# Half of the second pair's input loaded before the first pair's ticks, and an identity matrix loaded six ticks earlier

## The chip, the core and the metric

The kernel runs on one core of a Trainium2 chip. The metric is the device time of one execution in microseconds (us). The engines of the core are named as the profile names them: PE is the matrix engine (its weight loads are shown as PEld), DVE the vector engine, ACT the scalar engine, POOL and SP two more engines that here mainly issue DMA transfers. A `q` behind a name (SPq, POOLq) is the part of an engine that issues.

## The reference

What is computed, for `x` of 8 batch entries, 5696 positions and 128 channels:

```python
def _attn_ref(x, h):
    L = 2 * S
    Xf = np.fft.rfft(x, n=L, axis=1)
    Hf = np.fft.rfft(h, n=L, axis=0)
    return np.fft.irfft(Xf * Hf[None, :, :], n=L, axis=1)[:, :S, :]

def _moe_ref(x, w_r, w_i, w_ch):
    X = np.fft.rfft(x, axis=1)
    Y = np.zeros_like(X)
    Xr, Xi = np.real(X[:, :64]), np.imag(X[:, :64])
    Yr = einsum('bmd,mde->bme', Xr, w_r) - einsum('bmd,mde->bme', Xi, w_i)
    Yi = einsum('bmd,mde->bme', Xr, w_i) + einsum('bmd,mde->bme', Xi, w_r)
    Y[:, :64] = Yr + 1j * Yi
    u = x + np.fft.irfft(Y, n=S, axis=1)
    return u + np.maximum(u @ w_ch, 0.0)
```

The first function is a causal convolution along the sequence with one filter per channel. The second takes its result, multiplies the lowest 64 Fourier modes by a 128x128 complex matrix each, adds the inverse transform to the result, and ends with a residual ReLU product with `w_ch`. Inputs and output are float32; the kernel works in float16 with float32 accumulation.

## The kernel before

All transforms are matrix products. A position is split as s = 64 q + p, with 89 values of q and 64 of p. The spectrum is worked through in 90 classes; four classes make a tick, so a pass over all classes has 23 ticks (0 to 22). Two batch entries make a pair, and the program goes through four pairs one after the other.

**Input.** `Xin` holds the pair's x, with q on the partitions. It comes in eight pieces of 16 values of p each (`XN`), four for each of the two entries. A piece is brought from DRAM by two DMAs issued by POOL (`x_load`: 80 rows and 9 rows, float32 in DRAM and float16 on arrival) into a staging place, and then copied by one DVE instruction into `Xin` (`x_place`, L362), which can't happen before the last first-stage matmul of the pair before has read `Xin`. The first pair's pieces are staged as `Xr`, which lies over the first part of the tile `Hs`. The later pairs' pieces are staged as `Xt`, eight places that lie over the front of the tile `As`; piece i covers eight classes of it, those of ticks 2i and 2i + 1.

**First stage** (`a_tile`, 32 of them for each pair): products of `Xin` with `F`, moved out of PSUM into `As` by ACT and DVE in turn. A tile needs all of `Xin`. Six of the next pair's tiles are drawn into the last ticks of a pair (the table `border`), the first at tick 22.

**Ticks.** In tick t, `second` multiplies `As` with the constant `M` for four classes, ACT moves the result to `Xs`, DVE multiplies it by the filter's spectrum `Hs` into one of three buffers `U` (L617 and L625), PE multiplies the product of two ticks earlier by `Wc`, ACT moves that into a slot of `Zs` or `Zt`, SP writes the slot to DRAM (`zscr`), and PE multiplies a slot of one tick earlier by `G` for the 64 modes. During the first pair's ticks the filter's own spectrum is built too, six ticks ahead (`filter_tick`, `LH` = 6, so in ticks 0 to 16): PE makes it from `Ah` and `M`, DVE moves it into the first half of `Hs` (L312), and two DMAs issued by SP copy it, with its halves of partitions swapped, into the second half. The product of a tick needs all three to have arrived.

**Tick order.** Each engine's program is a list in the order in which the Python code adds to it, and every engine works its list strictly in order, SP's and POOL's DMA issues included. Waits are made from reads and writes of named tokens. In `tick(g_, t)` the order is: `x_place` of the pieces due at t, `second`, `products`, the loads for the next pair, the `Wc` products and the write to `zscr`, the `G` products, `filter_tick`.

**Input of the next pair, before the change.** At the even ticks 2 to 16 of a pair, piece t/2 - 1 is loaded into its place over `As`, after the tick's products and `second` are done. For the second pair the copies stand at ticks 9, 10, 12, 15, 16, 18, 20 and 22 of the first (`XPLACE[0]`).

**Last pair and after.** During the last pair's ticks the dictionary `early` issues loads for what follows: mode weights `W`, tables `S4a`, `S4b` and `IBs`, and chunks `ZT0` to `ZT3` read back from `zscr`. The identity matrix `Id` is loaded by SP at tick 20; its place lies over one of the `Zt` slots 8 and 9, which the last pair uses once only, at ticks 8 and 9, so it waits for those slots' readers (`after=ZY`). After the ticks PE mixes the modes (`XT` with `W`), DVE and ACT move the result to `Y`, PE transposes it with `Id` (L808), ACT and DVE move that to `C`, and then the output stage runs: per tile, products of `ZT` with `S4` and of `C` with `IBs` into `UT`, then products with `w_ch`, ReLU, sum, and writes of the output by SP.

Of the kernel before, what the change touches and what calls it, by code (L numbers as in the profile page):

```python
# [5 lines left out]
F16 = mybir.dt.float16  # L6
# [117 lines left out]
def bass_long_conv_fft__then__afno_spectral_mix_kernel(nc, x, h, moe_w_r, moe_w_i, moe_w_ch, out):  # L124
    B, S, D = x.shape
# [3 lines left out]
    NQ = S // J  # L129
    assert NQ * J == S  # L130
    L = 2 * S
    NK = NQ + 1
    NP = B // 2
    KT = 4
# [71 lines left out]
    def at(name, cols, dt, off):  # L206
        return nc.alloc_sbuf_tensor_at(name, [P, cols], dt, offset=off)
# [7 lines left out]
    AW, HW, GW = NK * 2 * D, NK * D, (NK // 2 + 1) * P  # L215
# [8 lines left out]
    a_h = take(2 * HW * 2)  # L224
# [4 lines left out]
    NU, NXS, NZ, NZX = 3, 2, 6, 10  # L229
# [7 lines left out]
    XC = 4  # L237
    XN = J // XC
    XB = XN * D
    x_all = at("Xr", 2 * XC * XB, F16, a_h)  # L240
    x_st = [at(f"Xt{i}", XB, F16, a_as + i * XB * 2) for i in range(2 * XC)]
    u_s = [at(f"U{i}", 2048, F16, a_st + i * 4096) for i in range(NU)]
    x_s = [at(f"Xs{i}", 1024, F16, a_st + NU * 4096 + i * 2048) for i in range(NXS)]
    z_s = [at(f"Zs{i}", 1024, F16, a_st + NU * 4096 + (NXS + i) * 2048) for i in range(NZ)] + \
# [44 lines left out]
    def pv(bank, off, dims, p0=0, n=P):  # L289
        return bass.AP(ps, p0 * 4096 + bank * 512 + off, [[4096, n]] + [list(d) for d in dims])  # L290
# [5 lines left out]
    def bank(i):  # L296
        return ("bank", i)
# [3 lines left out]
    def evac(dst, src, reads, writes, scale=None, eng=None, after=()):  # L301
        e = eng
        if e is None:
            turn[0] ^= 1
            e = "scalar" if turn[0] else "vector"
        if e == "scalar":
            if scale is None:
                R.add(e, lambda h_: h_.copy(dst, src), reads, writes, after=after)  # L308
            else:
                R.add(e, lambda h_: h_.activation(dst, src, COPY, scale=scale), reads, writes, after=after)  # L310
        elif scale is None:
            R.add(e, lambda h_: h_.tensor_copy(dst, src), reads, writes, after=after)  # L312
        else:
            R.add(e, lambda h_: h_.tensor_scalar_mul(dst, src, scale), reads, writes, after=after)  # L314
# [9 lines left out]
    def once(key, toks):  # L324
        if key in first:
            return []
        first[key] = 1
        return list(toks)
# [32 lines left out]
    def x_place(i, src, toks):  # L361
        R.add("vector", lambda e: e.tensor_copy(bass.AP(x_sb, i * XN * XS, [[XW, NQ], [XS, XN], [1, D]]),  # L362
                                                src),
              list(toks) + XZ, [("xin", i)])
# [107 lines left out]
             [bank(t), bank(t + 1)], [("as", j)], 1.0 / 64, eng=eng, after=once(("hp", j), HP))  # L472


    def filter_tick(t, banks):
        n = len(ticks[t])
        hb = banks
        for i, k in enumerate(ticks[t]):
            for r in range(2):
                for dh in range(2):  # L480
                    mm(pv(hb[dh], i * DH, [[1, DH]]),
                       ap(m_sb, MW, J * dh, J, k * 3 * J + (J if r == 0 else 0) + dh * J, [[1, P]]),
                       ap(ah_sb, HW, J * dh, J, (2 * k + r) * DH, [[1, DH]]), r == 0, r == 1,
                       AHT + mtok(k) + [("ag", k)], [bank(hb[dh])])
        lo, hi = KT * t * D, (KT * t + n) * D
        old = once("xr", [t_ for r_ in XR for t_ in r_]) if t == 0 else []
        evac(h_sb[:, lo:hi], pv(hb[0], 0, [[DH, n], [512, 2], [1, DH]]), [bank(hb[0]), bank(hb[1])], [("h", t, 0)],
             eng="scalar" if t < LH and t != 2 else "vector",
             after=old)
        for p0, p1 in ((0, J), (J, 0)):  # L490
            dma("sync", h_sb[p0:p0 + J, HW + lo:HW + hi], h_sb[p1:p1 + J, lo:hi], "s", [("h", t, 0)], [("h", t, 1, p0)])
        if t % 2 and t // 2 < NG:
            s0, s1 = t // 2 * GP, min(t // 2 * GP + GP, NS)
            dma("sync", g_sb[:, s0 * P:s1 * P], bass.AP(c_g, s0 * P, [[GW, P], [1, (s1 - s0) * P]]), "c", (),
                [("g", t // 2)], after=[("ag", k) for k in range(s0, s1)])
# [24 lines left out]
    def clear_zt(i):  # L520
        z32 = zt[i][1][0:PB, :].bitcast(U32)
        R.add("gpsimd", lambda e: e.memset(z32, 0), (), [("zt0", i)], after=list(zt_old[i][1]) + pace)
# [13 lines left out]
    def load_s4(part):  # L536
# [6 lines left out]
    early = {3: lambda: load_w(2), 5: lambda: load_w(3), 8: lambda: load_s4(1),  # L543
             10: lambda: clear_zt(0),
             11: lambda: load_zt(0, "gpsimd"),
             14: lambda: clear_zt(1),
             15: lambda: load_zt(1, "gpsimd"),
             16: lambda: load_s4(0),
             18: lambda: load_ib(),
             20: lambda: load_id(),  # L550
             NT - 2: lambda: (load_zt(2, "gpsimd", SLACK), load_zt(3, "gpsimd"), clear_zt(2), clear_zt(3))}
    pace = []
    SLACK = [("zd", NP - 1, s_) for s_ in range(NT - NZL)]
# [1 line left out]
    def load_id():  # L555
        dma("sync", id_sb[:, :], bass.AP(c_w, 2 * P, [[3 * P, P], [1, P]]), "c", (), [("id",)], after=ZY)
# [47 lines left out]
    def products(g_, t, sl):  # L604
# [15 lines left out]
        if not straight(g_, t):  # L620
            e = onchip.get((g_, t))
            if e is None:
# [2 lines left out]
        R.add("vector", lambda e: e.tensor_tensor(uv, src, hv, MULT),  # L625
              bk + [("h", t, 0), ("h", t, 1, 0), ("h", t, 1, J)], [("u", i)])

    Z_OLD = [("ag", k) for k in range(NS, NS + 8 * (NZX - NZ))]
    XPLACE = [9, 10, 12, 15, 16, 18, 20, 22], [9, 10, 13, 14, 17, 18, 20, 22]

    def zroom(g_, s_):
        if g_ == NP - 1:
            return s_ if s_ < NZX else (s_ - NZX) % NZL
        return (s_ - 2 * NZ) % NZX if g_ == 0 and s_ >= 2 * NZ else s_ % NZS[g_]

    def xtok(n):
        return [("xt", n, p_) for p_ in range(2)]

    def tick(g_, t):
        if g_ + 1 < NP:  # L640
            for i in range(2 * XC):
                if t == XPLACE[g_ > 0][i]:
                    x_place(i, bass.AP(x_st[i], 0, [[XB, NQ], [D, XN], [1, D]]), xtok(i))
        with_h = with_h_at(g_, t)
        if t < NT:
            of_two = t > 0 and twin(g_, t - 1)
            if not of_two:
                second(g_, t)
            products(g_, t, slot_of(g_, t))
            if twin(g_, t):  # L650
                second(g_, t + 1)
                if straight(g_, t):
                    copied(g_, t + 1, slot_of(g_, t + 1))
        drain = list(border[t]) if t in border and g_ + 1 < NP else []
        if drain and t >= NT:
            j, sl, e = drain.pop(0)
            a_tile(j, [sl], e)
        if g_ + 1 < NP and t % 2 == 0 and 0 < t <= 4 * XC:
            i = t // 2 - 1
            x_load(g_ + 1, i, x_st[i], xtok(i), [("u", t % NU)] + AST)  # L660
        if LC <= t < NT + LC:
            s_ = t - LC
            n = len(ticks[s_])
            i, zi = s_ % NU, zroom(g_, s_)
            zb = [turns("z", ZBANK) for b in range(2)]
            for b in range(2):
                for r in range(2):
                    mm(pv(zb[b], 0, [[1, n * D]]), (W1, W2)[r], u_s[i][:, r * 1024 + b * 512:r * 1024 + b * 512 + n * D],
                       r == 0, r == 1, [("u", i), ("wc",)], [bank(zb[b])])
                evac(bass.AP(z_s[zi], b * D, [[1024, P], [2 * D, n], [1, D]]),  # L670
                     pv(zb[b], 0, [[D, n], [1, D]]), [bank(zb[b])], [("zs", zi, b)], eng="scalar",
                     after=once(("zx", zi, b), Z_OLD) if zi >= NZ else ())
            zo = (g_ * NK + KT * s_) * P * 256
            dma("sync", bass.AP(zs, zo, [[256, P], [P * 256, n], [1, 256]]),
                bass.AP(z_s[zi], 0, [[1024, P], [256, n], [1, 256]]), "z",
                [("zs", zi, 0), ("zs", zi, 1)], [("zd", g_, s_)])
            if drain and t >= NT:
                j, sl, e = drain.pop(0)
                a_tile(j, [sl], e)
        if LM <= t < NT + LM:  # L680
            s_ = t - LM
            zi = zroom(g_, s_)
            for i, k in sorted(enumerate(ticks[s_]), key=lambda q: (s_ > 0 or q[1] != 1, q)):
                for b in range(2):
                    if k % 2:
                        o, off, n, sl = pv(MB, b * P, [[1, P]]), (k + 1) // 2 * P, P, (k + 1) // 2
                    else:
                        ms, off = even[k]
                        n, sl = 2 * len(ms), 0
                        dims = [[M, 2]] if len(ms) == 1 else [[ms[1] - ms[0], 2], [M, 2]]  # L690
                        o = pv(MB, b * P + ms[0], dims)
                    mm(o, z_s[zi][:, i * 256 + b * P:i * 256 + b * P + P], g_sb[:, off:off + n],
                       k == 1 and b == 0, k == NK - 1 and b == 1, [("g", sl // GP), ("zs", zi, b)], [bank(MB)])
        if drain and t < NT + LM - 1:
            j, sl, e = drain.pop(0)
            a_tile(j, [sl], e)
        if with_h:
            filter_tick(t + LH, [2, 3])

    FOUR = [0, 2, 4, 6]  # L700
    for j in range(32):
        a_tile(j, FOUR)
# [217 lines left out]
```

## Time and profile before

| | us |
|---|---|
| three timed executions | 385.3, 388.07, 394.62 |
| their median | 388.07 |
| the profiled execution | 392.56 |
| its span, first to last instruction | 390.3 |

The profiled execution's time is 2.26 us over its span; that remainder lies outside the instructions. Its mean granted clock was 0.981.

| engine | busy us | share of the span |
|---|---|---|
| PE | 361.9 | 93% |
| ACT | 310.9 | 80% |
| DVE | 303.4 | 78% |
| PEld | 278.7 | 71% |
| POOL | 84.8 | 22% |

In the trace the first pair's first stage runs from 27 to about 44 us, its ticks from there to about 93, the second pair's part to about 149, the third's to about 204, the fourth's ticks end at about 262, and the output stage runs from about 274 to the end. Busy time says where an engine works, not whether the end depends on it; for that the chain of work that ended last and the idle time before an instruction are read, stretch by stretch. A DMA is seen in two places: the issue on the queue of its engine, and the time at which it landed.

### The profile page before, as it was taken

To read this page: it belongs to the slowest core of one execution; us is meant where nothing else is said; L and a number is where in the kernel's file an instruction comes from. 1 tells how busy PE (TensorE), PEld (TensorE's weight loads), DVE (VectorE), ACT (ScalarE), POOL (GpSimd) and SP (SyncE) were. 2 spreads that over 40 slices of the span, in tenths; PEclk is the share of its full clock that TensorE was granted. 3 is DMA by queue.
4 is the path that set the end of the run, shared out by engine and by line. 5 is a ranking of instruction groups with operands and counts; after the bars stand their busy time and mean duration, and the time that the engine had idled before them with its cause. 6 is when DMAs were issued, how large, how long until landed. Compare 5 with 4: busy or idle time off the path is not lost.

```text
span 390.3 us, 12468 instructions
## 1 busy us (share of the span) xinstructions
PE 361.9 (93%) x5346; PEld 278.7 (71%) x5346; DVE 303.4 (78%) x346; ACT 310.9 (80%) x489; POOL 84.8 (22%) x134
## 2 busy tenths in 40 slices
PE   7889899988989999989999899995999999999993
PEld 7878766655856667856667666665898988988872
DVE  3649889977998998989999988763437767777785
ACT  8469599987889997899997899992457676777784
POOL 8700022310643210832213213346000000000000
PEclk9999999999999999999999999996899999999997
DMA  7997489998899996999995899999889999999767
GB/s 147 210 307 303 127 164 269 253 250 253 85 137 200 241 265 176 121 122 238 244 274 113 125 313 360 352 368 396 316 322 364 359 414 412 410 403 372 293 269 304
DMA packets 87202, 103.94 MB, mean 266 GB/s; under 512 B 22884, under 2 KB 72676, under 8 KB 83592
## 3 DMA queue, kind: packets, MB, share of 16 engines
q1 hardware_dynamic: 62667, 67.76, 50.3%
q0 software_dynamic: 24480, 35.40, 43.1%
q8 instruction: 42, 0.69, 0.7%
q14 instruction: 13, 0.10, 0.1%
HBM read 70.61 MB, written 51.12 MB: 312 GB/s over the span
## 4 chain that ended last, share of the span: by engine, by line
PE 67%; DMA 12%; DVE 7%; ACT 5%; POOL 3%; issue 2%; SPq 1%; DVEq 0%; POOLq 0%
PE ps L320 67%; DMA Xt<-in_x_dram 4%; DMA Xr<-in_x_dram 4%; DMA Id<-cW 3%; DVE As L314 2%; DVE U L617 2%; POOL Xr L317 2%; ACT As L310 2%; DMA Hs<-Hs 1%; ACT R L854 1%; SPq L317 1%; DVE Xin L362 1%; ACT UT L308 1%; POOL Hin L317 1%; DVE Hs L312 1%
## 5 line engine op out<-in xcount | busy, mean ns | idle before, releaser
L625 DVE TENSOR_TENSOR U<-Xs,Hs 128x2048 f16<-128x2048 f16 (+1 forms) x73 | 86.9, 1192 | 16.6 <-ACT Xs L308 12.9
L320 PE MATMUL ps<-U,Wc 128*128 128x512 f16 (+1 forms) x368 | 94.2, 376 | 0.6 <-DVE U L617 0.5
L308 ACT CAST Xs<-ps 128x1024 f16<-128x1024 f32 (+1 forms) x77 | 74.9, 977 | 12.3 <-PE ps L320 7.3
L308 ACT CAST Zs<-ps 128x512 f16<-128x512 f32 (+1 forms) x132 | 69.2, 595 | 3.3 <-PE ps L320 1.9
L855 DVE TENSOR_TENSOR O<-ps,R 128x512 f32<-128x512 f32 x81 | 52.5, 685 | 19.8 <-ACT R L854 12.6
L854 ACT ACTIVATE R<-ps 128x512 f32<-128x512 f32 x96 | 50.9, 573 | 14.3 <-PE ps L320 13.8
L314 DVE TENSOR_SCALAR As<-ps 128x720 f16<-128x720 f32 x70 | 57.7, 884 | 5.2 <-PE ps L320 4.6
L320 PE MATMUL ps<-F,Xin 128*128 128x180 f16 x512 | 53.7, 249 | 5.5 <-DVE Xin L362 4.2
L320 PE MATMUL ps<-As,M 64*128 64x128 f16 x1440 | 50.3, 217 | 5.1 <-DVE U L617 2.9
L320 PEld LDWEIGHTS ps<-F,Xin 128*128 128x128 f16 x512 | 44.4, 155 | 14.2 <-DVE Xin L362 2.9
L320 PE MATMUL ps<-WI,UT 128*128 128x256 f16 x360 | 51.8, 278 | 0.5 <-DVE O L855 0.4
L310 ACT ACTIVATE As<-ps 128x720 f16<-128x720 f32 (+1 forms) x61 | 45.7, 770 | 7.7 <-PE ps L320 6.3
L320 PEld LDWEIGHTS ps<-U,Wc 128*128 128x128 f16 x368 | 28.4, 97 | 29.9 <-ACT Zs L308 4.2
L320 PEld LDWEIGHTS ps<-As,M 64*128 64x128 f16 x1440 | 40.6, 94 | 11.3 <-DVE U L617 3.6
L317 POOL DMA_DIRECT2D Xt<-in_x_dram x48 | 25.9, 543 | 101.0 <-PE ps L320 95.5
L308 ACT CAST UT<-ps 128x712 f16<-128x712 f32 x40 | 30.0, 752 | 18.4 <-PE ps L320 17.5
L320 PEld LDWEIGHTS ps<-WI,UT 128*128 128x128 f16 x360 | 39.2, 152 | 4.2 <-issue 1.9
L320 PE MATMUL ps<-IBs,C 128*128 128x356 f16 x128 | 40.3, 324 | 0.6
L320 PEld LDWEIGHTS ps<-G,Zs 128*128 128x128 f16 x512 | 26.0, 96 | 14.6 <-ACT Zs L308 2.0
L625 DVE TENSOR_TENSOR U<-ps,Hs 128x2048 f16<-128x2048 f32 x15 | 34.2, 2283 | 0.0
L320 PE MATMUL ps<-G,Zs 128*128 128x128 f16 (+2 forms) x512 | 32.3, 192 | 0.1
L308 ACT CAST Zt<-ps 128x512 f16<-128x512 f32 x52 | 28.5, 620 | 1.9 <-PE ps L320 1.9
(86 smaller groups left out, 501.2 us busy)
## 6 DMA issues: line engine op xcount, KB each, us to landing
out_dram<-O SPq DMA_DIRECT2D x39, 512.0 KB, 7.5
zscr<-Zs SPq DMA_DIRECT2D x62, 256.0 KB, 7.4
Xt<-in_x_dram POOLq DMA_DIRECT2D x24, 320.0 KB, 7.2
zscr<-Zt SPq DMA_DIRECT2D x26, 256.0 KB, 6.5
W<-wscr POOLq DMA_DIRECT2D x4, 1024.0 KB, 7.9
M<-cM POOLq DMA_DIRECT2D x5, 720.0 KB, 17.0
ZT0a<-zscr SPq DMA_DIRECT2D x3, 1024.0 KB, 8.5
Hs<-Hs SPq DMA_DIRECT2D x44, 64.0 KB, 5.5
```

Source lines behind the costliest of these rows:

```text
L308: R.add(e, lambda h_: h_.copy(dst, src), reads, writes, after=after)
L310: R.add(e, lambda h_: h_.activation(dst, src, COPY, scale=scale), reads, writes, after=after)
L312: R.add(e, lambda h_: h_.tensor_copy(dst, src), reads, writes, after=after)
L314: R.add(e, lambda h_: h_.tensor_scalar_mul(dst, src, scale), reads, writes, after=after)
L317: R.add(eng, lambda h_: h_.dma_start(dst, src), reads, writes, ring=ring, after=after)
L320: R.add("tensor", lambda h_: h_.matmul(o, l, r, start=st, stop=sp), reads, writes)
L362: R.add("vector", lambda e: e.tensor_copy(bass.AP(x_sb, i * XN * XS, [[XW, NQ], [XS, XN], [1, D]]), src), list(toks) + XZ, [("xin", i)])
L617: R.add("vector", lambda e, b=b, s_=s_: e.tensor_tensor(bass.AP(u_s[i], b * 512, [[2048, P], [1024, 2], [1, n * D]]), s_, hv, MULT), [tok, ...
L625: R.add("vector", lambda e: e.tensor_tensor(uv, src, hv, MULT), bk + [("h", t, 0), ("h", t, 1, 0), ("h", t, 1, J)], [("u", i)])
L854: R.add("scalar", lambda e: e.activation(rv, src_r, RELU), bk, [("r", i % NR)], after=once(("r", i % NR), G_ALL + XTT + [("y", 0), ("y", 1 ...
L855: R.add("vector", lambda e: e.tensor_tensor(ov, src_u, rv, ADD), bk + [("r", i % NR)], [key + (h_,)], after=once(key, old))
```

## The change

There are three edits.

1. Four of the second pair's eight pieces get places `Xh` in `Hs`: pieces 0 and 1 over classes 58 to 73 of its two halves, pieces 2 and 3 over classes 74 to 89. Their eight DMAs are added to POOL's list behind the loads of `M` and ahead of anything of the first stage, and wait for the last copy out of `Xr`. The filter's own results for these classes (from `filter_tick` 14 and 18 on) wait until the pieces are copied.
2. The other four pieces go to the first four places over `As`, at ticks 3, 6, 9 and 12 (`XLATE`) instead of eight at ticks 2 to 16. The copies for the second pair stand at ticks 3, 5, 7, 9, 11, 14, 17 and 20. The third and fourth pairs' input is loaded and placed as before.
3. `load_id` goes from tick 20 to tick 14 of the last pair, ahead of the clearing of `ZT1b` (a POOL instruction) at the same tick.

```diff
--- before.py
+++ after.py
@@ -239,6 +239,9 @@
     XB = XN * D
     x_all = at("Xr", 2 * XC * XB, F16, a_h)
     x_st = [at(f"Xt{i}", XB, F16, a_as + i * XB * 2) for i in range(2 * XC)]
+    NXH = 4
+    KH = [NK - 2 * XN, NK - XN]
+    x_h = [at(f"Xh{i}", XB, F16, a_h + (i % 2 * HW + KH[i // 2] * D) * 2) for i in range(NXH)]
     u_s = [at(f"U{i}", 2048, F16, a_st + i * 4096) for i in range(NU)]
     x_s = [at(f"Xs{i}", 1024, F16, a_st + NU * 4096 + i * 2048) for i in range(NXS)]
     z_s = [at(f"Zs{i}", 1024, F16, a_st + NU * 4096 + (NXS + i) * 2048) for i in range(NZ)] + \
@@ -472,6 +475,14 @@
              [bank(t), bank(t + 1)], [("as", j)], 1.0 / 64, eng=eng, after=once(("hp", j), HP))
 
 
+    def xtok(n):
+        return [("xt", n, p_) for p_ in range(2)]
+
+    def x_room(g_, i):
+        if g_ > 1:
+            return x_st[i]
+        return x_h[i] if i < NXH else x_st[i - NXH]
+
     def filter_tick(t, banks):
         n = len(ticks[t])
         hb = banks
@@ -484,6 +495,9 @@
                        AHT + mtok(k) + [("ag", k)], [bank(hb[dh])])
         lo, hi = KT * t * D, (KT * t + n) * D
         old = once("xr", [t_ for r_ in XR for t_ in r_]) if t == 0 else []
+        for i in range(NXH):
+            if KT * t + n > KH[i // 2]:
+                old = old + once(("xh", i), xtok(i))
         evac(h_sb[:, lo:hi], pv(hb[0], 0, [[DH, n], [512, 2], [1, DH]]), [bank(hb[0]), bank(hb[1])], [("h", t, 0)],
              eng="scalar" if t < LH and t != 2 else "vector",
              after=old)
@@ -543,11 +557,10 @@
     early = {3: lambda: load_w(2), 5: lambda: load_w(3), 8: lambda: load_s4(1),
              10: lambda: clear_zt(0),
              11: lambda: load_zt(0, "gpsimd"),
-             14: lambda: clear_zt(1),
+             14: lambda: (load_id(), clear_zt(1)),
              15: lambda: load_zt(1, "gpsimd"),
              16: lambda: load_s4(0),
              18: lambda: load_ib(),
-             20: lambda: load_id(),
              NT - 2: lambda: (load_zt(2, "gpsimd", SLACK), load_zt(3, "gpsimd"), clear_zt(2), clear_zt(3))}
     pace = []
     SLACK = [("zd", NP - 1, s_) for s_ in range(NT - NZL)]
@@ -625,22 +638,20 @@
         R.add("vector", lambda e: e.tensor_tensor(uv, src, hv, MULT),
               bk + [("h", t, 0), ("h", t, 1, 0), ("h", t, 1, J)], [("u", i)])
 
+    XLATE = [3, 6, 9, 12]
     Z_OLD = [("ag", k) for k in range(NS, NS + 8 * (NZX - NZ))]
-    XPLACE = [9, 10, 12, 15, 16, 18, 20, 22], [9, 10, 13, 14, 17, 18, 20, 22]
+    XPLACE = [3, 5, 7, 9, 11, 14, 17, 20], [9, 10, 13, 14, 17, 18, 20, 22]
 
     def zroom(g_, s_):
         if g_ == NP - 1:
             return s_ if s_ < NZX else (s_ - NZX) % NZL
         return (s_ - 2 * NZ) % NZX if g_ == 0 and s_ >= 2 * NZ else s_ % NZS[g_]
 
-    def xtok(n):
-        return [("xt", n, p_) for p_ in range(2)]
-
     def tick(g_, t):
         if g_ + 1 < NP:
             for i in range(2 * XC):
                 if t == XPLACE[g_ > 0][i]:
-                    x_place(i, bass.AP(x_st[i], 0, [[XB, NQ], [D, XN], [1, D]]), xtok(i))
+                    x_place(i, bass.AP(x_room(g_ + 1, i), 0, [[XB, NQ], [D, XN], [1, D]]), xtok(i))
         with_h = with_h_at(g_, t)
         if t < NT:
             of_two = t > 0 and twin(g_, t - 1)
@@ -655,9 +666,12 @@
         if drain and t >= NT:
             j, sl, e = drain.pop(0)
             a_tile(j, [sl], e)
-        if g_ + 1 < NP and t % 2 == 0 and 0 < t <= 4 * XC:
-            i = t // 2 - 1
-            x_load(g_ + 1, i, x_st[i], xtok(i), [("u", t % NU)] + AST)
+        if g_ + 1 < NP:
+            i = t // 2 - 1 if t % 2 == 0 else -1
+            if g_ == 0:
+                i = XLATE.index(t) + NXH if t in XLATE else -1
+            if 0 <= i < 2 * XC:
+                x_load(g_ + 1, i, x_room(g_ + 1, i), xtok(i), [("u", t % NU)] + AST)
         if LC <= t < NT + LC:
             s_ = t - LC
             n = len(ticks[s_])
@@ -697,6 +711,8 @@
         if with_h:
             filter_tick(t + LH, [2, 3])
 
+    for i in range(NXH):
+        x_load(1, i, x_h[i], xtok(i), [t_ for r_ in XR for t_ in r_])
     FOUR = [0, 2, 4, 6]
     for j in range(32):
         a_tile(j, FOUR)
```

## The prediction

> **What bounds the kernel now.** I read first the chain that ended last on the page, by line:
>
> ```profile
> PE ps L320 67%; DMA Xt<-in_x_dram 4%; DMA Xr<-in_x_dram 4%; DMA Id<-cW 3%; DVE As L314 2%; DVE U L617 2%; POOL Xr L317 2%; ACT As L310 2%; DMA Hs<-Hs 1%; ACT R L854 1%; SPq L317 1%; DVE Xin L362 1%; ACT UT L308 1%; POOL Hin L317 1%; DVE Hs L312 1%
> ```
>
> Two thirds is PE work, which the change leaves alone. What it can remove is DMA waits, and two lie at its places: `Id`, and `Hs` with the copy into `Xin`. Second, the PE timeline, searched for idle time (in brackets, with what ended it) at the end of the first pair (two lines) and ahead of the transposes (one):
>
> ```profile
> 82.35 0.62 PE L320 MATMUL ps<-As,M 64*128 64x128 f16 x16 [1.57 <-DVE Hs L312]
> ...
> 93.28 0.85 PE L320 MATMUL ps<-F,Xin 128*128 128x180 f16 x8 [1.53 <-DVE Xin L362]
> ...
> 272.77 1.05 PE L808 MATMUL ps<-Id,Y 128*128 128x128 f16 x8 [4.50 <-DMA Id<-cW]
> ```
>
> The named releasers are the last link only, so third the chain in order of time behind 93.28 (start, us, what):
>
> ```profile
> 80.74 1.24 DVE U L625
> ...
> 86.97 5.40 DMA Hs<-Hs
> ...
> 92.54 0.69 DVE Xin L362
> 93.24 0.05 issue
> 93.28 3.72 PE ps L320 x36
> ```
>
> The eighth copy stands at tick 22 on DVE behind the product of tick 21, which started at 91.40, just after its swapped half of `Hs` had landed (91.21). The 1.57 has the same root: the product of tick 16 started at 80.74, when its `Hs` landed (80.66, issued 72.83: 7.8 us, against a median of 2.0 at 46 to 51); the last filter evacuation waits behind it on DVE and holds the bank that PE needs at 82.35.
>
> Fourth, stretches of the first pair: length, busy time by engine, granted clock, then the DMA engines' busy share and GB/s:
>
> ```profile
> 33.00:37.00 4.00, 3.90 (x77) 3.24 (x76) 3.51 (x5) 3.52 (x6) 0.00 (x0) 1.00 0.75 279
> 37.00:52.00 15.00, 13.88 (x274) 10.97 (x268) 12.33 (x15) 10.53 (x17) 0.57 (x2) 1.00 0.44 117
> 52.00:90.00 38.00, 36.33 (x711) 23.74 (x704) 33.40 (x39) 34.92 (x53) 8.23 (x15) 1.00 1.05 253
> ```
>
> From 52 to 90 the DMA engines are full; from 37 to 52 over half their time is free. So late `Hs` is a full DMA system.
>
> **Edit 1 and 2, the early pieces.** A piece's price: the first pair's eight landed between 12.9 and 26.3 us with nothing beside them, 13.4 / 8 = 1.7 us each. Four cost 6.7. They wait for the copy that ends at 26.98; POOL's eight issues take 0.5 to 0.6 each, 4.5 us, and POOL has nothing else until 51.4. In the queue they stand behind `M`, whose last part lands at 37.4, so they run from there, in 15 x 0.56 = 8.4 us of free DMA time, and land by about 44 to 46. They are needed at ticks 3, 5, 7 and 9, the first just before the product at 51.54: 5 us of cover. What they slow is `Hs` and `G` of the first ticks, by at most the later latency of some 6 us instead of 2 to 3; the filter runs six ticks ahead (12 us), so I cost that at nothing. Without that cover the early ticks would get the wait that ticks 16 to 22 have now.
>
> In the ticks, POOL's queue took 43.4% of 16 engines over 51 to 93, 18.2 us for eight pieces; SP's queue took 59.7%. Halving the first leaves 81%: no longer full. By tick 16 the old kernel had issued seven pieces, the new one has issued its last at tick 12, so 3 x 2.3 = 7 us of DMA time has gone from before the `Hs` that were late by 1 to 2 us. I expect the waits at 80.74, 91.40 and 92.4 to go. Next late is ACT: 1.86 us a tick (0.90 for `Xs`, 0.96 for two `Zs`) beside PE's 1.85, so no new idle time.
>
> DVE: the eight copies stay eight copies of 0.68 (0.60 in a stream, 63.54 to 64.14). Two ticks of product and filter evacuation take 2 x (1.14 + 0.60), with one copy 4.08, against two ticks of 2.08: a copy every second tick fits, by 0.08. Now two stand at ticks 9 and 10, and the step at 68.59 is 2.25 instead of 2.08. The filter's new wait on the copies costs nothing: both are DVE instructions, the copies ahead by three ticks. Its last copy at tick 20 leaves tick 22 free, so the first `a_tile` no longer waits for DVE.
>
> Sum: 1.57 + 1.53 = 3.10, plus 0.17, less about 0.3 for evacuations that close up behind. I take 2.9. Bounds: 0 if the waits only move, 3.4 with all small steps.
>
> **Edit 3, the identity.** In the trace SP issues `Id` at 259.39 and it lands 13.2 us later. At tick 14 it stands behind the write of tick 12's slot (issued 246.63, 0.36 long), so it goes out at 247.0, and lands as that write did (252.7), at the worst 13 us later at 260. The transposes are due when `Y` is out of PSUM (DVE, done at 268.40). Its new wait, for the readers of slots 8 and 9, is over: the write of slot 9 landed at 245.71. Queued behind it on SP is the next write at 248.59, 0.6 us after the issue's longest (0.96); POOL's clearing is another queue. Without that cover, a block on SP would delay writes whose slots come round after eight ticks (some 14 us).
>
> PE then goes on at 268.45 instead of 272.77: 4.3 us of wait removed. But the clock matters here (stretches as above):
>
> ```profile
> 263.00:265.60 2.60, 2.59 (x81) 2.60 (x82) 2.60 (x1) 2.28 (x2) 2.60 (x3) 1.00 1.09 409
> 265.60:267.50 1.90, 1.90 (x68) 1.90 (x66) 0.40 (x1) 0.44 (x1) 1.90 (x4) 0.69 1.00 383
> ...
> 268.30:272.70 4.40, 0.00 (x0) 0.00 (x0) 0.10 (x1) 0.00 (x0) 1.21 (x1) 0.50 1.05 390
> 272.70:276.40 3.70, 3.63 (x25) 2.63 (x26) 2.09 (x3) 1.36 (x3) 0.00 (x0) 0.50 0.91 349
> 276.40:281.00 4.60, 4.60 (x86) 4.10 (x85) 1.80 (x2) 2.00 (x3) 0.00 (x0) 0.98 0.89 288
> ```
>
> By these shares the clock fell to half at 266.3, before the wait began and with PE busy, and came back at 276.56, 3.8 us after PE resumed. If it comes back the same 3.8 us after PE goes on, everything moves by the whole wait: 4.3. If it stays half until 276.56 whatever PE does, 4.3 us more of the work runs at half clock (`S4` products 75 instead of 43 ns apart, a factor near 1.8) and the gain is 2.4. If it never falls, 2.0 + 3.8 us of slow work shrink by 1/1.8 as well: 4.3 + 2.5 = 6.8. I take 4.3, the row's own case.
>
> [...]
>
> Nothing behind waits in turn: `IBs` landed at 262.7, `ZT2` at 269.2 and is used from about 281, `ZT3` at 273.6 and from about 285, `ZT4` at 278.0 and from about 289, each with over 6 us where 4.3 are taken. From 274 on the chain is PE, so the gain reaches the end.
>
> **Sum.** 2.9 + 4.3 = 7.2 off the profiled execution's 392.56 (span 390.3 and 2.26 around it): 385.4. That execution is 4.5 above the median of 388.07; taken off the median, the forecast is 380.9.
>
> **Rivals.**
> - *The clock stays open.* [...] 2.9 + 6.8 = 9.7: 378.4.
> - *Only `Id` pays:* DMA stays full (81% is a mean, `zscr` writes come in bursts), ticks 16 to 22 wait as before, and 4.3 is won: 383.8.
> - *Only the first pair pays:* `Id` is early, but a transfer or the half clock takes the 4.3 back. The landings above speak against it, and 2.9 is won: 385.2.
> - *It doesn't do what it says:* shorter executions than the profiled one may lack these waits, and nothing is left to win: 388.
> - *Slower:* the early pieces land late. The copies of ticks 3 and 5 stand ahead of the products on DVE, so lateness past 51.5 goes straight into the ticks, and every engine waits. It decides from a landing of 51.5 + 7.2 = 58.7 on; a landing at 67 costs 15.5 and gives 388.1 + 15.5 - 7.2 = 396.4. The slowest piece of the trace took 8.0 us, which speaks against it.
>
> **Chances.** Forecast case 0.53 (own range 378 to 384), clock open 0.20, only `Id` 0.08, only the first pair 0.08, nothing 0.04, slower 0.07. Beyond 2% (380.3 and 395.8, about what a measurement of this kernel can tell from no change) faster: 0.27 of the forecast case, which straddles the bound, and the open clock, 0.47. Slower: 0.04 of the last. Within: 0.49. The range leaves out the last two cases and the ends: below, gains of 3.4 + 6.8 give 377.9, and a median of a few runs that spread by 9 us is unsteady by some 1.5, so 376.4; above, 385.2 + 1.4 = 386.6.
>
> **What would show it.** Right: no PE idle over 0.5 us at 78 to 94 and none before L808; `Hs` landings near tick 20 under 5 us; DMA share after 52 under 1; `Id` landed before 262. Wrong: DVE idle before the copies of ticks 3 or 5; PE idle behind L808 for `ZT` or `IBs`; the clock at half until the same length after it fell.

## The result and the profile after

The changed kernel's median is 385.96 us over 22 executions (383.62 to 388.69), that of the kernel before in the same rounds 390.09 us over 22 (385.3 to 399.71). The ratio is 0.992, with a 95% interval of 0.9898 to 0.9943; it leaves out executions over 1.5% above the fastest of the same kernel, which takes long ones from before and none from after, so the means below say more. All executions of all rounds together, in us:

| kernel | executions | mean | median | standard deviation |
|---|---|---|---|---|
| before | 155 | 391.6 | 390.8 | 3.6 |
| changed | 64 | 386.4 | 386.4 | 1.7 |

The change is worth 5.3 us by the means (with a standard error of 0.4) and 4.4 by the medians, and it halves the spread: 72 of the 155 executions of before took over 391.1 us, none of the 64 changed ones did. The forecast was 380.9 within 376.4 to 386.6: faster was right, inside the range too, but the gain was put at 7.2.

The two profiled executions differ by just what was forecast: 392.56 - 385.31 = 7.25. That is partly luck: the one of before was 0.9 us above the mean of its kernel, the one after 1.1 below. The profile after, in the views that were read before. The chain that ended last, by line:

```profile
PE ps L323 73%; DMA Xr<-in_x_dram 4%; DVE As L317 2%; DMA Xt<-in_x_dram 2%; DVE U L630 2%; POOL Xr L320 2%; ACT As L313 2%; ACT R L870 1%; ACT Zs L311 1%; ACT UT L311 1%; POOL Hin L320 1%; DVE Xin L365 1%; DVE Hs L315 1%; ACT Zt L311 1%; ACT Xs L311 1%
```

The DMAs of `Id` and `Hs` are gone from it, and the share of `Xt` has halved. The PE timeline at the two places:

```profile
89.80 0.49 PE L323 MATMUL ps<-G,Zt 128*128 128x4 f16 x8
90.12 0.80 PE L323 MATMUL ps<-F,Xin 128*128 128x180 f16 x8
...
265.30 1.04 PE L824 MATMUL ps<-Id,Y 128*128 128x128 f16 x8 [0.49 <-issue]
```

The second pair's first tile follows the `G` products with no idle time and starts at 90.12 instead of 93.28, although this execution was 0.43 us later than the other when its ticks began. The transposes wait for nothing but their issue, and start 7.47 us earlier. Of the 7.25 us, the first pair's ticks up to that tile gave 3.6 (forecast: 2.9) and the stretch from there to the transposes 4.3 (forecast: 4.3); the later start of the ticks and an output stage that took 0.4 us longer took 0.8 back. Stretches of the first pair (length, busy time by engine, clock, DMA share, GB/s):

```profile
33.00:37.00 4.00, 3.96 (x66) 3.32 (x64) 3.46 (x5) 3.56 (x6) 0.00 (x0) 1.00 1.04 338
37.00:52.00 15.00, 13.81 (x256) 10.77 (x256) 12.40 (x16) 10.49 (x17) 0.00 (x0) 1.00 0.83 205
52.00:90.00 38.00, 37.83 (x739) 24.95 (x739) 35.36 (x41) 36.69 (x58) 4.38 (x8) 1.00 0.92 231
```

The DMA work has moved from the third row to the second (0.44 to 0.83, 1.05 to 0.92), and PE is busy 37.83 of 38 us instead of 36.33.

### The profile page after: what moved, and what is told of

It is laid out like the page before. It is cut to its first block, busy times and chain, and to the rows that moved or that the text cites. A ratio compares the mean times of both kernels' runs of the same rounds, so it can differ in the third digit from the quotient of the medians.

```text
span 383.2 us, 12465 instructions
## 1 busy us (share of the span) xinstructions
PE 360.0 (94%) x5346; PEld 277.7 (72%) x5346; DVE 303.1 (79%) x346; ACT 310.7 (81%) x489; POOL 84.4 (22%) x134
## 4 chain that ended last, share of the span: by engine, by line
PE 73%; DVE 7%; DMA 6%; ACT 6%; issue 3%; POOL 3%; DVEq 0%; POOLq 0%
PE ps L323 73%; DMA Xr<-in_x_dram 4%; DVE As L317 2%; DMA Xt<-in_x_dram 2%; DVE U L630 2%; POOL Xr L320 2%; ACT As L313 2%; ACT R L870 1%; ACT Zs L311 1%; ACT UT L311 1%; POOL Hin L320 1%; DVE Xin L365 1%; DVE Hs L315 1%; ACT Zt L311 1%; ACT Xs L311 1%
## 5 line engine op out<-in xcount | busy, mean ns | idle before, releaser
L320 POOL DMA_DIRECT2D Xt<-in_x_dram x40 | 21.4, 540 | 80.3 <-PE ps L323 79.8
```

The costliest lines, as they stand in the source:

```text
L320: R.add(eng, lambda h_: h_.dma_start(dst, src), reads, writes, ring=ring, after=after)
```

## The experiments

The question was where some 2 to 3 us had gone between the traces (7.25) and the executions. The kernel before ran beside each set of these kernels, with means of 391.2 to 391.6 us, so means of different sets are compared; that of 12 executions has a standard error of 0.4 to 0.9 us. First the two parts were taken apart, and both whole kernels profiled again.

**The kernel before, again** (no edit).

> The kernel before, unchanged, for a second profile. The profiles of before and after differ by 7.25 us, as summed, but the medians of 22 runs by 4.1 only. Theory 1 (the first profile of before was an execution with longer DMA waits than most): the second profile is nearer to 388, and of the three PE waits (1.57, 1.53 and 4.50 us) about 3 us are missing in all. Theory 2 (the profile was typical, and the new kernel loses 3 us in most executions but not in its profile): the second profile shows the same three waits at nearly the same size.

Mean 393.2 in 12 executions. The profile, an execution of 397.04 us, was not nearer to 388 but had a wait for `Id` of twice the size. PE timeline:

```profile
277.19 1.05 PE L808 MATMUL ps<-Id,Y 128*128 128x128 f16 x8 [9.30 <-DMA Id<-cW]
```

The first pair's waits were a little smaller here (0.64, 0.27, 1.46 and 0.37, 2.7 in all against 3.1). `Id` was issued at 259.39 as before and landed 17.7 us later instead of 13.2. The two profiles of one kernel differ by 4.48 us, and this wait by 4.80. So a wait that the forecast took as a fixed term varies by its own size; neither theory had that, the first expecting it smaller in a second profile and the second nearly the same.

**Edit 3 alone.**

```diff
-             14: lambda: clear_zt(1),
+             14: lambda: (load_id(), clear_zt(1)),
-             20: lambda: load_id(),
```

> Edit 3 alone: Id at tick 14, the pieces as before. Theory 1a (the wait for Id is the one that most executions lack): under 1.5 us faster than before, ratio above 0.996. Theory 1b (the first pair's waits are the ones that most lack): 3 to 4.5 us faster, ratio 0.988 to 0.992. Its profile shows Id landed by 262 and no PE idle time before the transposes, and the first pair's waits as in whichever execution is profiled.

Mean 389.5, median 389.3 (12): 2.1 us under the mean of all executions of before, 1.5 under their median, ratio 0.9937 (0.9891 to 0.9983): between the two theories. Its profile had no wait for `Id`, but two things that the first profile of the changed kernel lacks. SP's timeline:

```profile
244.90 2.26 SPq L317 DMA_DIRECT2D zscr<-Zs  x2
251.25 0.33 SPq L317 DMA_DIRECT2D Id<-cW  x1
251.62 3.06 SPq L317 DMA_DIRECT2D zscr<-Zs  x3
```

SP stood for 4.1 us at the load of `Id`, until slot 9's write had landed at 251.23, and then ACT for a slot of its own:

```profile
263.35 1.66 ACT L308 CAST Zs<-ps 128x512 f16<-128x512 f32 x4 [2.98 <-DMA zscr<-Zs]
```

**Edits 1 and 2 alone** (the changed kernel with the lines of edit 3 turned back).

> Edits 1 and 2 alone: the pieces early, Id at tick 20. Theory 1a: 2.5 to 3.2 us faster than before, ratio 0.992 to 0.994, and the profile has an Id wait below 2 us. Theory 1b: under 1.5 us faster, ratio above 0.996, and the profile has the Id wait of 4 us or more. If the two parts give 7 us together when taken alone, the loss is between them.

Mean 388.9, median 388.0 (12), 2.7 us under the mean of before, ratio 0.9934 (0.9887 to 0.9981): the size of theory 1a, but not its reason, since the profile has a wait for `Id` of 5.75 us and the spread is still 3.0:

```profile
271.72 1.05 PE L825 MATMUL ps<-Id,Y 128*128 128x128 f16 x8 [5.75 <-DMA Id<-cW]
```

**The changed kernel, again** (no edit).

> The changed kernel, unchanged, timed beside the two halves on one chip and profiled a second time. Expected under theories 1a and 1b alike: 3 to 4.5 us faster than before, ratio 0.989 to 0.993, no PE idle time over 0.5 us from 78 to 91 us and none before the transposes. Theory 2: a wait of some 3 us that the first profile of this kernel did not have.

Mean 386.6 (12), ratio 0.9933 (0.9897 to 0.997). The means add up: 2.7 for the pieces and 2.1 for `Id` against 5.0 for both here, so within the 1 us or so that these means can tell, nothing is lost between the parts. In this profile PE stood 2.27 us at the last `G` products, for ACT, which had waited 2.37 for a slot. That made a theory of its own: what `Id` wins is partly given back because SP stands at its load. Three kernels tested it.

**`Id` in the place of `F`,** loaded at tick 1 of the last pair:

```diff
-    id_sb = at("Id", P, F16, r_off[1])
+    id_sb = at("Id", P, F16, a_f1)
-        dma("sync", ..., "c", (), [("id",)], after=ZY)
+        dma("sync", ..., "c", (), [("id",)], after=[("f1",)])
-             14: lambda: (load_id(), clear_zt(1)),
+             1: lambda: load_id(), ..., 14: lambda: clear_zt(1),
```

(The output stage's later use of that place waits for `Id` as well; that line is left out here.)

> The changed kernel with Id in the place of F, which the last pair's ticks no longer use, loaded at tick 1 of the last pair: no wait of SP for the slots 8 and 9, and no load of Id among the last ticks. Theory A (part of what Id wins is given back because SP stands at the load of Id until slot 9's write has landed, so that later slot writes go out late and ACT waits for a slot): 1 to 2 us faster than the changed kernel, mean near 385, and no PE idle time over 0.5 us from 255 to 264. Theory B (the slot wait comes from full DMA engines with or without Id): same as the changed kernel within 0.5 us, and in some profiles a PE wait of 2 to 3 us for ACT Zs near the last tick.

**`Id` at tick 16.**

> The changed kernel with Id loaded at tick 16 instead of 14, when slot 9's write has landed in every trace so far. Theory A: SP doesn't stand; 0.5 to 1.5 us faster than the changed kernel unless Id now lands after 265 (issued near 248 it should land by 262). Theory B: same as the changed kernel.

**`Id` at tick 12.**

> The changed kernel with Id at tick 12, one tick after slot 9 is written out: the suspected wait of SP made longer, to 4 to 6 us in every execution (slot 9's write is issued near 238.4 and lands 4 to 9 us later, Id's turn comes near 240). Theory A: a slot wait of 2 to 5 us on ACT near the last ticks in the profile, and 1.5 to 4 us slower than the changed kernel. Theory B: same as the changed kernel within 1 us; SP catches up before the slots come round.

**The changed kernel beside them.**

> The changed kernel once more, on the chip and in the rounds of the three kernels before, as the measure for them: mean near 386.4. In its profile, Id's issue on SP later than the end of the issue ahead of it by 0 to 4 us, and if by over 2 us, a slot wait of ACT near the last tick.

Means of 12 each: in the place of `F` 385.6, tick 16 386.7, tick 12 386.7, changed 386.8. With `Id` at tick 12 SP stood 3.1 us (242.18 to 245.28), and it cost nothing that these rounds show; ACT's slot wait in its profile was 0.9. That speaks against theory A. Only the kernel without any late load came out lower, by 1.2 us, as theory A wanted.

**The kernel before with `Id` in the place of `F`** (the same edit on the other kernel).

> The kernel before with only Id moved into the place of F and loaded at tick 1 of the last pair, the pieces as before: the wait for Id taken away whole, with nothing put in its place. The profiles of before show waits of 4.5 and 9.3 us, but these are two executions out of a spread of 385 to 400. If the typical execution has the 4.3 us that were forecast: mean 4 us or more under that of before, near 387.4. If the wait is a tail (0 to 2 us in half of the executions, 5 to 10 in some): mean 2 to 3.3 us lower, median 1 to 2.5 us lower, and the spread of the times falls from some 3.5 us (standard deviation) to about 2.

Mean 388.3, median 387.9, standard deviation 1.6 (12). This is the price of the whole wait in the executions: 3.4 us by the mean and 2.9 by the median of all executions of before (3.3 and 3.2 by those of its own rounds), between the two cases of the expectation, and with it goes most of the spread of the kernel before. Its profile has the first pair's waits, smaller than in the first profile of before, and 0.23 us of issue ahead of the transposes. PE timeline:

```profile
81.56 0.62 PE L321 MATMUL ps<-As,M 64*128 64x128 f16 x16 [1.09 <-DVE Hs L313]
...
91.44 0.85 PE L321 MATMUL ps<-F,Xin 128*128 128x180 f16 x8 [0.79 <-DVE Xin L363]
...
266.48 1.05 PE L808 MATMUL ps<-Id,Y 128*128 128x128 f16 x8 [0.23 <-issue]
```

**`Id` in the place of `F`, a second and a third time, and the changed kernel beside them.**

> The changed kernel with Id in the place of F, again, beside the changed kernel: mean 0.5 to 1.5 us under it if the load of Id at tick 14 gives back a part at SP or in the DMA queue; equal within 0.4 if the first comparison was chance.

> The changed kernel, as the measure beside the three: mean 386.1 to 386.8 in the runs so far, some 5 us under the mean of before (391.4) and 4 us under its median.

> Id in the place of F, loaded at tick 1, beside the changed kernel on one chip: mean 0.5 to 1.2 us under it, if the difference of the first 18 and 52 executions (385.5 and 386.3) is one.

> The changed kernel, as the measure beside the three: mean 386.3.

Means 385.3 (6) against 385.7 (6), then 386.1 (12) against 386.5 (12): both differences of 0.4. Over all rounds it is 385.75 (30, standard error 0.27) against 386.36 (64, 0.21): 0.6 us lower, by 1.8 standard errors. It is the lowest mean of the versions with 12 executions or more, but not one that is shown to beat the changed kernel. And the third profile settles what the slot wait is not. ACT's timeline, with `Id` loaded at 217 us and out of the way:

```profile
257.05 1.07 ACT L312 CAST Zs<-ps 128x512 f16<-128x512 f32 x2 [0.44 <-DMA zscr<-Zs]
260.42 0.65 ACT L312 CAST Zs<-ps 128x256 f16<-128x256 f32 x2 [2.30 <-DMA zscr<-Zs]
```

The same wait for a slot, without a load of `Id` anywhere near: it ended when slot writes landed that had taken 12 and 14 us, with the DMA engines' busy share at 1.02 from 245 to 261 us.

**`Id` in the place of `F`, but at tick 14,** so without the wait for slots 8 and 9.

> Id in the place of F, but loaded at tick 14 as in the changed kernel: the same load at the same turn on SP, without the wait for slots 8 and 9. If SP's standing gives back the 0.8 us that lie between the changed kernel (mean 386.3) and Id at tick 1 (385.5): mean as with Id at tick 1. If it is the load itself among the last ticks, or chance: mean as the changed kernel.

Mean 386.4 (12), as the changed kernel's 386.4; its profile has a slot wait of 2.11 us with SP not standing. ACT's timeline:

```profile
260.71 0.65 ACT L312 CAST Zs<-ps 128x256 f16<-128x256 f32 x2 [2.11 <-DMA zscr<-Zs]
```

So the slot wait does not need SP to stand, no cost of SP's new wait shows in the means, and theory A falls as the account of it. That SP's standing adds nothing at all is not shown: of the changed kernel's five profiles, the two in which SP stood (0.6 and 1.8 us) are the two with the slot wait.

**Why `Id` is late: `ZT3` behind the loads of `WI`** (pieces early, `Id` at tick 20).

```diff
-             NT - 2: lambda: (load_zt(2, "gpsimd", SLACK), load_zt(3, "gpsimd"), clear_zt(2), clear_zt(3))}
+             NT - 2: lambda: (load_zt(2, "gpsimd", SLACK), clear_zt(2))}
...
-    for i in range(4, NC):
+    for i in range(3, NC):
```

> Pieces early, Id at tick 20, and the loads of ZT3 (1.4 MB) taken from ahead of the loads of WI, at tick 21, to behind them: the DMA engines then have less queued in the time in which Id is on its way. If Id is late because its queue shares full engines with those loads, it lands 2 to 4 us sooner than in the other profiles with Id at tick 20 (13 to 18 us after its issue), and the mean falls by 1 to 2.5 us from that of the pieces alone, to about 2.7 + 1.5 = 4 us under before. If it is late because of the slot writes ahead of it on SP's own queue, nothing changes: 2.7 us under before, Id landing 13 us or more after issue. A risk beside both: ZT3 arrives late, PE idle time near 280 to 290.

In its profile `Id` landed 7.9 us after its issue and PE did not wait; but the mean was 388.6 and the standard deviation 3.0, as with the pieces alone (388.9 and 3.0). One good execution was profiled and the long ones are still there: it doesn't decide.

**`Id` issued by POOL at tick 20** (pieces early).

```diff
-        dma("sync", id_sb[:, :], ..., "c", (), [("id",)], after=ZY)
+        dma("gpsimd", id_sb[:, :], ..., "p", (), [("id",)], after=ZY)
```

> Pieces early and Id at tick 20 as in the run with the pieces alone (mean 388.9, standard deviation 3.0), but issued by POOL, whose list has no slot writes, ahead of the loads of ZT2 and ZT3. If Id is late for the writes ahead of it on SP's queue: it lands under 9 us after its issue, the long executions go (standard deviation under 2), and the mean falls by 2 to 3.4 us, to 385.5 to 387. If it is late for full DMA engines whatever the queue: mean within 1 us of 388.9, landing 13 us or more after issue, spread unchanged.

Mean 385.3, standard deviation 1.4 (6), and `Id` landed 8.2 us after its issue. The view of the tile `Id`:

```profile
L320 POOL DMA_DIRECT2D Id<-cW x1: 542/542/542, 251.1 to 251.1; - x1
```

This is the first of the two cases expected: 3.6 us under the mean of the pieces alone, with a standard error of about 1. It is not a clean proof of the queue: POOL came to the load at 251.1 and SP at 256 to 259, because SP's list has the slot writes of ticks 16 to 20 ahead of it. Place in SP's list and place in its DMA queue were changed together; both say that `Id` was late for what stood ahead of it on SP, and how much each has of it stays open.

## Why the prediction was right about the waits and wrong about what one of them is worth

- **What bounds it, and the first pair's root (full DMA, late `Hs`):** right. Over 79 to 88 us `Hs` now lands in 1.9 to 4.2 us. A rest of the wait, 0.66 and 0.39 us at 81 us, is left in two of the 14 profiles with the pieces early.
- **The early pieces:** right. Forecast to land by 44 to 46, landed between 38.3 and 46.7; no copy waited for data, and the profile puts no idle time of PE down to them. (PE's new 0.17 us at 54.28 is put down to DVE's evacuation of `Hs`.) DVE's timeline in the changed kernel's profile, with the first two copies in their places at ticks 3 and 5:

```profile
51.21 0.68 DVE L315 CAST Hs<-ps 128x512 f16<-128x512 f32 x1
51.81 0.68 DVE L365 COPY Xin<-Xh 89x2048 f16<-89x2048 f16 x1
52.41 1.21 DVE L638 TENSOR_TENSOR U<-Xs,Hs 128x2048 f16<-128x2048 f16 x1
53.55 0.68 DVE L315 CAST Hs<-ps 128x512 f16<-128x512 f32 x1
54.15 1.21 DVE L638 TENSOR_TENSOR U<-Xs,Hs 128x2048 f16<-128x2048 f16 x1
55.28 0.68 DVE L315 CAST Hs<-ps 128x512 f16<-128x512 f32 x1
55.88 0.68 DVE L365 COPY Xin<-Xh 89x2048 f16<-89x2048 f16 x1
```

  From copy to copy it is 4.07 us, the forecast's 4.08, with nothing in brackets. One thing the forecast did not have: PE stands 0.41 to 0.90 us near 69 us in four of the 14 profiles with the pieces early (three of them of the changed kernel, none the first), and in none of the four without. The profile names no releaser, and the cause stays open.
- **The first pair's term, 2.9 us:** right. 2.7 (standard error 0.9) from before to the pieces alone, 2.5 (0.5) between the two kernels with `Id` in the place of `F`. In the traces, from PE's first wait of the ticks (45.47 us in the first profile of before) to the second pair's first tile it is 46.3 to 47.8 us in the four without the early pieces and 44.2 to 45.3 in the 14 with them.
- **`Id` lands before 262:** right, 249.4 in the first profile. "Its new wait ... is over" held in three of the changed kernel's five profiles; SP stood 1.8 and 0.6 us in the other two, and 4.1 with edit 3 alone. No cost of it shows in the means.
- **"I take 4.3", for `Id`:** the step that failed. The 4.3 is the wait in one execution. Taken away whole (`Id` in the place of `F`) it is worth 3.4 us in the mean and 2.9 in the median; profiles show 4.5, 5.75, 9.3 and none. The changed kernel gets 2.1 to 2.6 of that, each with a standard error of 0.8 to 0.9.
- **"Taken off the median":** the other failure. The median of three executions was 388.07; that of 155 is 390.8. The profiled execution, at 392.56, is 0.9 above the mean of all, not 4.5 above a typical one. In the rounds of the result the miss of 5.1 us is 2.0 of that (390.09 against 388.07) and 3.1 of gain (7.2 against 4.1).
- **The rivals:** "shorter executions than the profiled one may lack these waits" was given 0.04. It was true of a part, the wait for `Id`, and a rival for that part alone, with the spread of 385.3 to 394.6 as its evidence, was missing. The open clock did not come: no run shows what would keep it open, and in the profile after it was half for 3.4 us. Nor did the late pieces.
- **What is late next:** the forecast looked behind the transposes, where PE waited for no DMA. The next wait lies ahead of them: ACT for a `Zs` slot at the last ticks, 0.9 to 3.0 us, in 6 of the 13 profiles that have `Id` early and in none of the four that have it on SP at tick 20. It costs more than its length: from the second pair's first tile to the transposes it is 177.8 to 179.1 us in these six and 175.1 to 175.5 in the nine with neither this wait nor one for `Id`, some 3.3 us. Over the 13 that is 1.5 us in the mean, about the distance of 0.8 to 1.3 between what the edit won and the 3.4 of the whole wait. But one of the three profiles of the changed kernel with `Id` in the place of `F` from tick 1 has it too, so this account is argued and not shown. In each of the six, SP's issue of one of two `Zt` writes at 250 to 260 us took 2.7 to 4.8 us, where it took 0.36 in the other twelve profiles; what held it up is open.

## What to carry to other kernels

A wait on a DMA in one trace is a sample, not a term. Where a kernel's executions spread as those of before did (385.3 to 399.71 us), ask first which waits could make that spread, take a second profile before summing, and price such a wait by removing it in timed executions. A small transfer that many steps wait for did better here in a quiet stretch: in the place of `F`, `Id` went out near 217 us, where the DMA engines' share was 0.07 (217 to 219 us), and landed in 1.7 us; most of the spread went along with the mean.

## What the runs showed of the hardware

Near the mode mixing the granted clock was half for 3.4 to 13.6 us. Around the fall and the return, in the changed kernel's profile and in the second one of before (length, busy times, clock, DMA share, GB/s):

```profile
262.40:264.80 2.40, 2.40 (x76) 2.27 (x73) 0.69 (x2) 0.44 (x1) 2.40 (x5) 1.00 1.02 418
264.80:268.20 3.40, 2.91 (x22) 2.22 (x22) 2.22 (x4) 0.62 (x2) 1.51 (x1) 0.50 1.03 388
268.20:272.00 3.80, 3.80 (x67) 3.27 (x66) 1.65 (x3) 2.13 (x3) 0.00 (x0) 1.00 1.02 372
```

```profile
262.90:266.30 3.40, 3.40 (x113) 3.40 (x110) 2.73 (x1) 2.45 (x2) 3.40 (x5) 1.00 1.03 408
266.30:280.00 13.70, 4.40 (x63) 3.61 (x60) 2.41 (x4) 0.60 (x1) 2.83 (x3) 0.50 0.82 301
280.00:284.00 4.00, 4.00 (x72) 3.44 (x70) 1.92 (x3) 2.16 (x3) 0.00 (x0) 1.00 0.44 131
```

In this profile of the changed kernel the half clock lasted 3.4 us (in its others 3.4 to 10.2); with a wait for `Id` of 4.5 or 5.75 us 10.2, with 9.3 us 13.6. In the profiles without that wait it lasted 3.4 or 6.8, and 10.2 to 13.6 where PE stood 2 to 3 us for a slot. These lengths are near one, two, three and four times 3.4 us. What made the clock fall and what brought it back is not shown. In these two profiles no idle time of PE is seen just ahead of the fall: in the second block the clock fell after 3.40 us of a PE shown busy throughout, and in the changed kernel's it did the same (busy 3.40 of the 3.40 us from 261.40 to 264.80, in part in products with 16 columns).

What the half clock is longer by with a wait for `Id` lies for the most part in the wait itself and not behind it: outside the waits of 4.5, 5.75 and 9.3 us it lasted 5.7, 4.5 and 4.3. From the transposes to the end it took 117.6 to 117.7 us in the three profiles with a wait for `Id` and 116.1 to 118.2 in the other 15, so no half-clock time behind the wait is seen to be saved with it. The clock came back 3.8 us after PE went on before the change and 2.9 us after it; in this pair the forecast's case, that it comes back about as long after PE as before, held.
